# Raw V and R begun in one run behind psat, and two places of hand order made plain

## The chip, the cores and the metric

The kernel runs on one core of one Trainium2 chip. TensorE (PE; its weight loads are shown apart as PEld), the vector engine (DVE), ScalarE (ACT) and GpSimd (POOL) work beside each other, each through its own list of instructions; transfers are begun by a queue, here nearly always that of SyncE (SP), and carried out by 16 DMA engines. Engines wait for each other by semaphores. The metric is the device time of one execution in microseconds (us); a kernel's time is the median of its runs.

## The reference

Two blocks follow each other. The first is a recurrence over 768 steps for 4 batches and 8 heads with a state of 40 x 40; the second a mixture of four small networks over 3072 tokens.

```python
for t in range(S):                                   # B, H, S, D = 4, 8, 768, 40
    y[:, :, t] = einsum('bhd,bhde->bhe', r_t, state)
    Sa = einsum('bhde,bhe->bhd', state, a_t)
    state = state * w_t[:, :, None, :] - einsum('bhd,bhe->bhde', Sa, b_t)
    state = state + einsum('bhd,bhe->bhde', v_t, k_t)
x = y.transpose(0, 2, 1, 3).reshape(3072, 320)
p = probs / (probs.sum(-1) + 1e-9)
for e in range(4):
    out += p[:, e] * (relu(x @ w1[e]) @ w2[e])       # w1 320 x 1024, w2 1024 x 320
```

## The kernel before

**Units.** The 768 steps are cut into 12 chunks of 64; the four batches go two by two. A chunk of one pair is a unit, and there are 24, numbered u = 2 * chunk + pair. Within a unit the recurrence is written as matrix products; only a small state passes from a chunk to the next. The loop over u at line 1142 works on four units at once: it finishes unit u (`s`, from `step`), merges unit u+1 (`m`, from `merge`), prepares unit u+2 (`w`, from `within`) and loads unit u+3. `run(gen, n)` advances such a generator by n of its `yield`s.

**The parts of a unit, by the names in the profile.**
- `load_raw` (L206) begins the transfers of W, A, V and R in a blocked form (rawW, rawA, rawV, rawR, one buffer each); L223 is the line of the transfers. V and R take 8 moves each, 16 in all. They are put in a list, `later`, and begun from there by `begin_later`. `load` (L198) brings natW, natB, natK and natV.
- `within` (L402): DVE turns rawW into G (L241) and scans it (L439, then gl at L443), computes gp, its reciprocal, n_tok (L471) and k_tok (L476), turns rawA, rawV and rawR into AT, VT and RT (L241). PE transposes n_tok and k_tok (pNT, pKT, L79), and forms pfe, pc, pe, pev; ACT copies pfe to F (L506).
- `substitute` (L544) takes F into `blocks`, turns it into M (L555 to L571, DVE), and solves a triangular system by 16 rounds of multiply and add on POOL, in Z (L576 to L595).
- `merge` (L601): DVE turns Z into Qc (L606) and Qc into QTc (L608), POOL copies QTc to QT (L614), PE forms pY (from QTc) and pQ, ACT copies Yq and QT (L629).
- `step` (L638): prn and the copies RH (DVE, L656) and SN (ACT, L661); psat, SaT and SX; pxr, whose result DVE masks into SX (L400); pdy; Y (L733 and L738) and the state (L743, L744) on DVE; and the twelve SP transfers that lay Y out as the rows of x, xT (L762). `psat` is formed by the `run(s_next, 1)` at line 1238.

**The mixture.** A list `todo` holds its pieces: an `Up` is one half of x @ w1[e] (ph, 16 small and 16 large matmul records, then the ReLU to hs on ACT, L799), a down piece is a group of products with w2 or sums of it (p431, p75, p26, named p in the profile), added into osb by DVE (L833, L835). `add_h` forms the sums a of hs on DVE (L932). The weights w1p have two buffers; `used` begins the next load when a piece is done (L300). Channels 256 to 319 of x, the last ones, are the smaller tiles (`up_last`), the rest is `up_main`. An `Up` can be called (`lead`, that is the last channels first, then the main ones) or split into `begin` (main ones) and `end` (last channels, ReLU), with other work between. Two units with the same chunk share the pieces; only units 0 and 1 have their own (`mixture_of_unit`, L845). PE's accumulators for all of these share three PSUM banks (tag mm); the others share five (tag big).

**What sets the order.** Instructions of PE are kept in program order (`stated`, L70). On DVE, POOL and SP those marked `keep_in_program_order` keep their order among the marked ones; the others (Y, gp, RT, VT among them) are placed by a scheduler by its own estimate of when they can run. So a transfer's place in the program can change where DVE's instructions stand. [...]

**Where V and R are begun.** `mix(n)` (L1005) runs n pieces and begins three moves of `later` after each, or six after each if n is 1. In the main loop (u from 5 on) the 16 moves of a unit are appended at line 1222; the mix(2) at L1233 begins 6, the mix(2) at L1243 another 6, and the mix(2) at L1209 of the next pass the last 4. They are used by `turn_rv` in that next pass. In the passes with u below 5 the line `begin_later(len(later))` stands at the pass's start (L1159).

Of the kernel before, what the change touches and what calls it, by code (L numbers as in the profile page):

```python
# [15 lines left out]
def kernel(  # L16
# [58 lines left out]
    def matmul(**k):  # L75
        return stated(nc.tensor.matmul(**k))  # L76
# [158 lines left out]
    def go(moves, eng=None):  # L235
        for move in moves:
            move(eng or nc.sync)
# [65 lines left out]
    def used(n):  # L303

        while len(pieces) < n_pieces:
            k = len(pieces)
            if k in in_sums:
                before = k - 5 if k >= 5 else -1
            else:
                at = [x for x in range(k) if x not in in_sums]  # L310
                before = at[-2] if len(at) > 1 else -1
            if before >= n:
                break
            load_piece()

    def load_w2(e):
        tc.keep_in_program_order(nc.sync.dma_start(out=w2_sb[e][:], in_=moe_w2[e].rearrange("(f p) d -> p f d", p=P)))
# [451 lines left out]
    def up_banks(n):  # L769
        return [ps.tile([P, HF // 2, n], FP32, name="ph", tag="mm", bufs=3) for _ in range(2)]  # L770

    def up_last(k, xT, ph, opens):

        w1 = pieces[k]
        for f in range(HF // 2):
            for c in range(2):
                for i in range(2):
                    matmul(
                        out=ph[i][half(c), f, :], lhsT=w1.last[part(i), f, half(c)], rhs=xT[part(i), 2, :],
                        start=(opens and f == 0), stop=(not opens and f == HF // 2 - 1),  # L780
                    )
# [22 lines left out]
    class Up:  # L804
# [4 lines left out]
        def lead(self):  # L809
            if self.ph is None:  # L810
                self.ph = up_banks(self.n)
                up_last(*self.at, self.ph, True)
# [14 lines left out]
    def scale(q, e, minus=False):  # L827
        return (minus_gate if minus else gate)[:, q.c, q.bp, e:e + 1]

    def add(to, p, sc, start=False):  # L830

        if start:
            nc.vector.tensor_scalar(out=to, in0=p, scalar1=sc, scalar2=None, op0=ALU.mult)  # L833
        else:
            nc.vector.scalar_tensor_tensor(out=to, in0=p, scalar=sc, in1=to, op0=ALU.mult, op1=ALU.add)  # L835

    def store(q, osb, cols=slice(0, DM), second=nc.sync):
        for i, eng in enumerate((nc.sync, second)):
            row = q.b[i] * S + q.c * L
            eng.dma_start(out=out[row:row + L, cols], in_=osb[i * L:(i + 1) * L, cols])  # L840

    def outputs():
        return sb.tile([P, DM], FP32, name="osb", tag="osb", bufs=2)

    def mixture_of_unit(q):  # L845

        hs, at = {}, 2 * E * q.u

        def ups(e):
            hs[e] = []  # L850
            a, b = (Up(at + 2 * e + x, q.xT, P, hs[e].append) for x in range(2))

            def piece():
                a()
                b.begin()
                b.end()
                used(at + 2 * e + 2)
                if q.u == 0 and e + 2 < E:
                    load_w2(e + 2)

            piece.lead = a.lead
            return piece

        def down(e):
            po = ps.tile([P, DM], FP32, name="po", tag="mm", bufs=3)
            for f in range(NF):
                matmul(
                    out=po[:], lhsT=hs[e][f // HF][:, f % HF, 0:P], rhs=w2_sb[e][:, f, :],
                    start=(f == 0), stop=(f == NF - 1),
                )  # L870
            if e == 0:
                q.osb = outputs()
            add(q.osb[:], po[:], scale(q, e), e == 0)
            if e == E - 1:
                stores.append(lambda: store(q, q.osb))

        todo.append(ups(0))
        for e in range(E):
            todo.append(lambda e=e: down(e))
            if e + 1 < E:  # L880
                todo.append(ups(e + 1))
# [116 lines left out]
    todo, last, later, stores = [], [], [], []  # L998

    def begin_later(n):  # L1000
        for move in later[:n]:
            tc.keep_in_program_order(move(nc.sync))
        del later[:n]

    def mix(n):  # L1005

        for piece in todo[:n]:
            ready = stores[:]
            del stores[:]
            piece()  # L1010
            for begin_store in ready:
                begin_store()
            begin_later(3 if n > 1 else 6)
        del todo[:n]
# [5 lines left out]
    def open_next():  # L1020
        if not todo:
            return None
        piece = todo.pop(0)
        piece.begin()
        return piece

    def run(gen, n=99):
        if gen is None:
            return
        for _ in range(n):  # L1030
            if next(gen, gen) is gen:
                break
# [109 lines left out]
    for u in range(1, NU):  # L1142
        in_order[0] = True
        q = units[u]
        m = s_next = w = w_next = iter(())
        if u + 1 < NU:
            m, s_next = merge(units[u + 1]), begin_step(u + 1)
            w_next = ws[u + 1]
        if u + 2 < NU:
            w = ws[u + 2]  # L1150

        def gap(n, pieces=None):
            at = 4 * u + n
            run(sum_ops, sums_at.get(at, 0))
            mix((1 if at in sparse else 2) if pieces is None else pieces)

        early = u < EARLY
        if early:
            begin_later(len(later))  # L1159
            lead()  # L1160
            run(w_next)
            run(s, 1)
            gap(0)
            run(s, 1)
            run(w, 2)
            gap(1, 2 if u + 1 == EARLY else None)
            run(s)
            if u == 1:
                mixture_of_unit(q)
            elif q.bp:  # L1170
                mixture_of_chunk(units[u - 1:u + 1], chunks_x[q.c])
            go(load_raw(begin(u + 3), "WA"))
            load(units[u + 3], "WBKV")
            later.extend(load_raw(units[u + 3], "VR"))
            run(w, 2)
            soon = u > 1
            if soon:
                run(w, 1)
            run(m, 1)
            if soon:  # L1180
                substitute(units[u + 2], nc.gpsimd)
            gap(2)
            if not soon:
                run(w, 1)
                substitute(units[u + 2], nc.gpsimd)
            run(w, 1)
            ws.append(within(units[u + 3]))
            run(ws[u + 3], 1)
            run(m, 1)
            run(s_next, 1)  # L1190
            run(m)
            gap(3, 1)
            run(s_next, 1)
            s = s_next
            continue

        ahead = u + 3 < NU and u < EARLY + 3
        if ahead:
            go(load_raw(begin(u + 3), "W"))
        if u == EARLY:  # L1200
            run(w_next)
            lead()
        run(s, 1)
        run(w_next)
        lead()
        run(s)
        run(sum_ops, sums_at.get(4 * u, 0))
        run(w, 1)
        mix(2)  # L1209
        if q.bp:  # L1210
            mixture_of_chunk(units[u - 1:u + 1], chunks_x[q.c])
        begin_later(len(later))
        run(w, 1)
        run(m, 1)
        run(sum_ops, sums_at.get(4 * u + 1, 0))
        up = open_next()
        run(w, 1)
        mix(1)
        if u + 3 < NU:
            go(load_raw(units[u + 3] if ahead else begin(u + 3), "A" if ahead else "WA"))  # L1220
            load(units[u + 3], "WBKV")
            later.extend(load_raw(units[u + 3], "VR"))

        if up:
            up.end()
        run(s_next, 1)
        run(m, 1)
        run(w, 1)
        lead()
        if u + 2 < NU:  # L1230
            substitute(units[u + 2], nc.gpsimd)
        run(sum_ops, sums_at.get(4 * u + 2, 0))
        mix(2)  # L1233

        run(m, 1)
        run(w, 2)
        lead()
        run(s_next, 1)
        if u + 3 < NU:
            ws.append(within(units[u + 3]))  # L1240
            run(ws[u + 3], 1)
        todo[:2] = todo[1::-1]
        mix(2)  # L1243
        s = s_next
    while todo:
        mix(2)
        up = open_next()
        mix(1)
        if up:
            up.end()  # L1250
            lead()
    for piece in last:
        piece()

# [27 lines left out]
```

## Time and profile before

| | us |
|---|---|
| median of 3 runs | 1165.82 |
| range of the runs | 1164.3 to 1168.21 |
| profiled execution | 1169.21 |
| span of its trace | 1167.5 |
| PE busy | 1082.7 |
| DVE busy | 747.0 |
| POOL busy | 487.9 |

The span runs from the first to the last instruction of the profiled execution; the rest of its time lies around it. Busy times are of one engine, and they overlap. The groups of the page that concern the change are these; a row is line, engine, operation, output<-inputs, shapes and count, then busy us and mean ns of one, then the idle us just before them and what ended them:

```profile
L76 PE MATMUL ph<-xT,w1p 64*64 64x256 f32 (+3 forms) x3040 | 449.3, 385 | 6.2 <-PE ph L76 2.8
L582 POOL TENSOR_TENSOR Z<-M,Z 128x62 f32<-128x62 f32 (+7 forms) x352 | 160.6, 456 | 95.3 <-DVE M L571 69.5
L614 POOL COPY QT<-QTc 32x256 f32<-32x256 f32 x96 | 40.5, 422 | 331.3 <-DVE QTc L608 327.6
L76 PE MATMUL pY<-QTc,below 64*64 64x64 f32 x384 | 18.2, 240 | 37.8 <-DVE QTc L608 37.8
```

Idle time counts only on the engine that bounds the kernel; POOL's 331.3 us before QT are of no harm by themselves, PE's 37.8 us before pY may be. SPq and PEq stand for the queue of an engine (issuing or waiting), and "issue" is time in which an engine waited for nothing that the profile shows.

### The profile page before, as it was taken

To read this page: it belongs to the slowest core of one execution; us is meant where nothing else is said; L and a number is where in the kernel's file an instruction comes from. 1 tells how busy PE (TensorE), PEld (TensorE's weight loads), DVE (VectorE), ACT (ScalarE), POOL (GpSimd) and SP (SyncE) were. 2 spreads that over 40 slices of the span, in tenths; PEclk is the share of its full clock that TensorE was granted. 3 is DMA by queue.
4 is the path that set the end of the run, shared out by engine and by line. 5 is a ranking of instruction groups with operands and counts; after the bars stand their busy time and mean duration, and the time that the engine had idled before them with its cause. 6 is when DMAs were issued, how large, how long until landed. Compare 5 with 4: busy or idle time off the path is not lost.

```text
span 1167.5 us, 38490 instructions
## 1 busy us (share of the span) xinstructions
PE 1082.7 (93%) x16102; PEld 971.3 (83%) x16102; DVE 747.0 (64%) x1551; ACT 354.4 (30%) x956; POOL 487.9 (42%) x1274
## 2 busy tenths in 40 slices
PE   7789999989899899899899989989989999999998
PEld 6677788888789798798888878988978988898887
DVE  8766678797566665766668557766666675543343
ACT  2331434422224233233332233233232422321110
POOL 4116677745436245264362452643633624600000
PEclk8898999999899899999999999999999999999999
DMA  6875544542534434334344344354353342222220
GB/s 113 252 218 121 135 100 106 111 117 57 126 86 112 113 83 119 95 84 119 93 106 113 79 101 116 77 129 111 82 125 88 104 118 61 70 87 76 79 91 12
DMA packets 268868, 122.18 MB, mean 105 GB/s; under 512 B 213736, under 2 KB 242072, under 8 KB 268696
## 3 DMA queue, kind: packets, MB, share of 16 engines
q1 hardware_dynamic: 265416, 119.12, 40.5%
q8 instruction: 127, 2.08, 0.7%
q10 hardware_dynamic: 3280, 0.61, 0.3%
q14 instruction: 45, 0.37, 0.1%
HBM read 111.79 MB, written 3.93 MB: 99 GB/s over the span
## 4 chain that ended last, share of the span: by engine, by line
PE 61%; SPq 18%; DVE 12%; issue 4%; DMA 4%; ACT 1%; DVEq 0%; ACTq 0%
PE ph L76 26%; PE p L76 19%; SPq L762 10%; PE pdy L76 3%; SPq L223 3%; SPq L300 2%; DMA rawR<-in_r_dram 2%; PE psat L76 2%; PE pxr L76 2%; SPq L840 2%; PE pfe L76 1%; PE pY L76 1%; PE pQ L76 1%; PE po L76 1%; PE pc L76 1%
## 5 line engine op out<-in xcount | busy, mean ns | idle before, releaser
L76 PE MATMUL ph<-xT,w1p 64*64 64x256 f32 (+3 forms) x3040 | 449.3, 385 | 6.2 <-PE ph L76 2.8
L76 PEld LDWEIGHTS ph<-xT,w1p 128*128 128x128 f32 (+1 forms) x3040 | 341.8, 165 | 65.8 <-issue 16.3
L595 POOL TENSOR_TENSOR Z<-Z 128x31 f32<-128x31 f32 (+7 forms) x704 | 241.2, 343 | 55.2
L799 ACT ACTIVATE hs<-ph 128x512 f32<-128x512 f32 (+1 forms) x208 | 113.8, 564 | 384.5 <-PE ph L76 372.9
L582 POOL TENSOR_TENSOR Z<-M,Z 128x62 f32<-128x62 f32 (+7 forms) x352 | 160.6, 456 | 95.3 <-DVE M L571 69.5
L614 POOL COPY QT<-QTc 32x256 f32<-32x256 f32 x96 | 40.5, 422 | 331.3 <-DVE QTc L608 327.6
L932 DVE TENSOR_TENSOR a<-hs 128x512 f32<-128x512 f32 x220 | 147.8, 689 | 47.8 <-ACT hs L799 47.8
L76 PE MATMUL p<-sums,a 128*128 128x160 f32 x1056 | 164.9, 299 | 0.0
L835 DVE SCALAR_TENSOR_TENSOR osb<-p,gate,osb 128x320 f32<-128x320 f32 (+1 forms) x243 | 107.7, 478 | 83.9 <-PE p L76 81.8
L76 PEld LDWEIGHTS p<-sums,a 128*128 128x128 f32 x1056 | 152.8, 190 | 2.2
L76 PE MATMUL p<-w,hs 128*128 128x160 f32 x704 | 104.9, 302 | 0.6 <-DVE osb L835 0.6
L76 PE MATMUL p<-w,a 128*128 128x160 f32 x704 | 102.8, 299 | 0.0
L76 PEld LDWEIGHTS p<-w,hs 128*128 128x128 f32 x704 | 97.3, 190 | 2.3 <-issue 1.0
L76 PEld LDWEIGHTS p<-w,a 128*128 128x128 f32 x704 | 98.0, 190 | 0.0
L400 DVE COPY_PREDICATED SX<-mask_up,pxr 128x256 f32<-128x256 int32 x48 | 18.8, 442 | 60.2 <-PE pxr L76 60.2
L733 DVE TENSOR_TENSOR Y<-pdy,RS 128x256 f32<-128x256 f32 x44 | 16.7, 420 | 61.8 <-PE pdy L76 60.6
L457 ACT COPY NT<-pNT 128x512 f32<-128x512 f32 x24 | 14.1, 586 | 136.3 <-PE pNT L79 136.0
L76 PE MATMUL pY<-QTc,below 64*64 64x64 f32 x384 | 18.2, 240 | 37.8 <-DVE QTc L608 37.8
L451 DVE RECIPROCAL gp<-gp 128x320 f32<-128x320 f32 x24 | 51.4, 2142 | 0.1
L629 ACT COPY QT<-pQ 32x128 f32<-32x128 f32 x96 | 24.7, 257 | 82.2 <-PE pQ L76 81.1
L555 DVE STREAM_TRANSPOSE M<-blocks 128x1024 f32<-128x1024 f32 x24 | 47.3, 1971 | 3.0 <-ACT blocks L549 2.6
L76 PEld LDWEIGHTS pY<-QTc,below 64*64 64x64 f32 x384 | 15.4, 150 | 40.6 <-issue 39.7
(149 smaller groups left out, 1377.7 us busy)
## 6 DMA issues: line engine op xcount, KB each, us to landing
w1p<-in_moe_w_dram SPq DMA_DIRECT2D x95, 512.0 KB
w1p<-in_moe_w_dram SPq DMA_DIRECT2D x190, 64.0 KB
w<-in_moe_w_dram SPq DMA_DIRECT2D x4, 1280.0 KB
sums<-in_moe_w_dram SPq DMA_DIRECT2D x9, 512.0 KB
natW<-in_w_dram SPq DMA_DIRECT2D x48, 80.0 KB
natB<-in_b_dram SPq DMA_DIRECT2D x48, 80.0 KB
natK<-in_k_dram SPq DMA_DIRECT2D x48, 80.0 KB
out_dram<-osb SPq DMA_DIRECT2D x46, 80.0 KB
```

The source lines that it names most:

```text
L76: return stated(nc.tensor.matmul(**k))
L223: moves.append(lambda eng, out=t[o, n, 0:w_], in_=heads[:, hs, Q * y:Q * y + w_]: eng.dma_start(out=out, in_=in_))
L451: pin(nc.vector.reciprocal(out=gp[:], in_=gp[:]))
L555: ins = nc.vector.transpose(out=M[:], in_=cols)
L582: ins = eng.tensor_tensor(out=Z[:, 1:3, 0:n, j + 1:Q], in0=M[:, j:j + 2, None, j + 1:Q].to_broadcast([P, 2, n, m]), in1=Z[:, here, 0:n, j: ...
L595: eng.tensor_tensor(out=z[:, 0], in0=z[:, 0], in1=z[:, x], op=ALU.add)
L614: ins = nc.gpsimd.tensor_copy(out=q.QT[quarter(i), :, quarter(i % 2)], in_=QTc[quarter(i)])
L629: nc.scalar.copy(out=of_slot(to[quarter(2 * r)], y), in_=src)
L762: nc.sync.dma_start(out=xT[to:to + hi - lo, g, :], in_=Y[at:at + hi - lo, h // 2].rearrange("p i t -> p (i t)"),)
L799: nc.scalar.activation(out=h[:, i * HF // 2:(i + 1) * HF // 2, 0:n], in_=ph[i][:], func=ACTF.Relu,)
L835: nc.vector.scalar_tensor_tensor(out=to, in0=p, scalar=sc, in1=to, op0=ALU.mult, op1=ALU.add)
L932: nc.vector.tensor_tensor(out=t[:], in0=x, in1=y, op=op)
```

## The change

Three edits:
- In `mixture_of_unit` the second `Up` of a piece is called (last channels, then the main ones) where it was begun and ended (main ones, then the last channels).
- In the main loop, u from 5 on, all that is left in `later` is begun behind psat, that is ahead of the last mix(2) of the pass; so V's and R's 16 moves are all begun in one pass, and used in the next.
- The pieces left when the loop is over run in the order of the list, each `Up` called; before, every third was begun, another piece run, and then ended, with the last channels of the next one right behind.

```diff
@@ mixture_of_unit, ups, piece() (L853)
                 a()
-                b.begin()
-                b.end()
+                b()
                 used(at + 2 * e + 2)
@@ main loop (L1239)
         if u + 3 < NU:
             ws.append(within(units[u + 3]))
             run(ws[u + 3], 1)
+        begin_later(len(later))
         todo[:2] = todo[1::-1]
         mix(2)
         s = s_next
-    while todo:
-        mix(2)
-        up = open_next()
-        mix(1)
-        if up:
-            up.end()
-            lead()
+    mix(len(todo))
     for piece in last:
         piece()
```

`begin_later(n)` begins the first n moves of `later` on SP, each kept in program order, and takes them off the list.

## The prediction

> **What bounds the kernel now.** I read the page first (busy shares), then who waited for whom on TensorE (PE), then the timeline of one step of the main loop, then its queue view for the next step. The page says that PE is the bound as a whole: it is busy 1082.7 us of 1167.5. So only its 85 us of idle time can be won. The view of waits says where almost half of that idle time is.
>
> ```profile
> PE 1082.7 (93%) x16102; PEld 971.3 (83%) x16102; DVE 747.0 (64%) x1551; ACT 354.4 (30%) x956; POOL 487.9 (42%) x1274
> ...
> PE pY L76 <- DVE QTc L608: 37.8, 16, 5.4
> ...
> PE ph L76 <- PE ph L76: 2.8, 4, 0.7
> ```
>
> Sixteen times PE stands before pY until the vector engine (DVE) has turned QTc: 37.8 us. The step at 512 to 545 us shows why. Each row is start, duration, engine, line, names, and in brackets the idle time before it and what ended it.
>
> ```profile
> 512.33 0.78 DVE L400 COPY_PREDICATED SX<-mask_up,pxr 128x256 f32<-128x256 int32 x2 [2.95 <-PE pxr L76]
> 515.92 0.76 DVE L733 TENSOR_TENSOR Y<-pdy,RS 128x256 f32<-128x256 f32 x2 [2.81 <-PE pdy L76]
> 517.67 0.51 POOL L595 TENSOR_TENSOR Z<-Z 128x8 f32<-128x8 f32 x2
> 525.60 0.48 DVE L476 TENSOR_TENSOR k_tok<-natK,gp 128x320 f32<-128x320 f32 x1
> 527.93 0.60 PE L79 MATMUL pKT<-ident,k_tok 128*128 128x128 f32 x4
> 529.60 0.17 DVE L443 TENSOR_TENSOR gl<-gl,G 128x8 f32<-128x8 f32 x1
> 533.09 0.71 DVE L241 STREAM_TRANSPOSE RT<-rawR 128x512 f32<-128x512 f32 x1 [3.32 <-DMA rawR<-in_r_dram]
> 533.73 0.57 DVE L606 STREAM_TRANSPOSE Qc<-Z 128x256 f32<-128x256 f32 x1
> 534.34 0.45 DVE L608 STREAM_TRANSPOSE QTc<-Qc 128x256 f32<-128x256 f32 x1
> 534.93 0.59 PE L76 MATMUL pY<-QTc,below 64*64 64x64 f32 x13 [1.18 <-DVE QTc L608]
> 538.14 0.65 ACT L506 COPY F<-pfe 128x256 f32<-128x256 f32 x2
> 542.55 0.69 DVE L571 TENSOR_TENSOR M<-M,Z 128x512 f32<-128x512 f32 x1
> ...
> 564.53 0.52 POOL L595 TENSOR_TENSOR Z<-Z 128x8 f32<-128x8 f32 x2
> ```
>
> The raw R that DVE turns at 533.09 has been begun too late; DVE idles 3.32 us for it, and Qc and QTc stand behind it. The reader should also see two things that cost nothing yet: GpSimd (POOL) finishes Z, which Qc reads, only at 518.18, that is 2.3 us after Y has begun; and M at 543.24 is followed by a POOL chain that ends at 565.05. In the next step (560 to 581 us) the queue view adds this:
>
> ```profile
> 572.01 1.66 SPq L300 DMA_DIRECT2D w1p<-in_moe_w_dram  x3
> 573.72 1.53 SPq L223 DMA_DIRECT2D rawR<-in_r_dram  x3
> 575.36 2.45 SPq L840 DMA_DIRECT2D out_dram<-osb  x4
> ...
> 578.14 0.55 DVE L833 TENSOR_SCALAR osb<-p,gate 128x320 f32<-128x320 f32 x1 [3.73 <-DMA out_dram<-osb]
> ```
>
> In every second step DVE also waits for the output stores, since osb is written anew.
>
> [...] Qc's input Z was ready at 518.18, yet Qc ran at 533.73, right behind RT. [...] SP's 12 xT moves (L762) start only at 562.63, after Y of 560.56, and the stores stand behind them. [...] Here the POOL chain from M to Z's end takes 25.3 us where DVE adds the w2 sums (213.88 to 239.20) and 21.4 to 21.9 us later[...].
>
> **The change part by part.**
>
> *1. Raw V and R begun ahead.* Before, of the 16 moves per unit 12 go out in the two mix(2) at a step's end and 4 a step later. After, all 16 go out before the last mix, so the last four R moves (about 0.5 us each) leave SP some 20 us earlier, and R lands before the next step's SX. RT can then run as soon as its buffer is free, after pxr. From the built program I read the order of DVE: in the 16 steps from the Qc of 300.0 us to that of 990.6 us, RT, Qc and QTc now stand between SX and Y; before, they stood behind gl (L443). PE, ACT and POOL keep their order in these steps. That removes the wait before pY: 37.8 less the 2.35 us of the one at 251 us, so 35.4 us.
>
> *What is late next.* Qc needs Z. DVE now stops at Qc until POOL ends, and Y, the state, gp, n_tok, k_tok and all that follows stand behind it. In the steps from 370 us on Z ends 2.0 to 4.5 us after Y's present start. This closes a loop: Z end, Qc, QTc, Y, k_tok, pKT, pfe, F, M, the next Z. Its price, link by link:
> - Z's end to Y: Qc starts 0.03 us after Z (112.68 to 112.71 in an early step); from Qc's start to what follows QTc is 534.70 − 533.73 = 0.97. Sum 1.0.
> - Y's start to k_tok's end: 526.08 − 515.92 = 10.16. DVE has no gap in it, and it is 10.15 to 10.26 in the 15 steps from 278 to 929 us, so nothing of it shrinks.
> - k_tok to pKT's end: 0.75, from the one step where PE really waited for it (243.07 to 243.82).
> - pKT's end to F's end: 7.9, from the step with no wait before pY (987.88 to 995.78). It holds the p431 products, the last-channel products, prn, pY, pfe.
> - F to M: 4.46 in every step. M to Z's end: 21.8.
>
> That is 46.1 us a turn. In every second step the stores come between: xT goes out from Y+2.1, w1p from Y+11.1 (median of the rows), the stores from Y+12.8 once the three R moves no longer stand before them, and the first osb follows 2.8 us behind its store's issue, at Y+15.6; the second 1.5 us later at Y+17.1. The rest of osb takes 1.2, so RH starts at Y+18.3. The ACT copies SN wait for RH and stand before F, which ends 2.6 us after RH's start (536.17 to 538.79), at Y+20.9 against Y+18.8 in the other steps. With 4.46, 21.6 and 1.0 the turn is 48.0 us. A mean of 47.05.
>
> Before, from the SX end of 325.44 to that of 971.40, 14 steps took 46.14 each, of which about 2.1 were the wait before pY. So PE would need 44.0, but the loop asks for 47.05. Walking it: Y of the first changed step starts at 281.50 + 1.0 = 282.5 (278.05 before). Fifteen turns follow, eight of 48.0 and seven of 46.1, less 0.3 for a first chain of 21.33: the last of these Y starts at about 988.6 (973.66 before), and its pfe ends 10.16 + 0.75 + 6.2 later at 1005.7 (994.03 before). So part 1 costs +11.7 us. PE's idle time moves from pY to pKT, and to the ph whose bank waits for DVE's osb.
>
> SP: the ten moved DMAs take about 5 us of issue, between the V moves and the next w1p. In the window at 550 to 557 us SP is idle for 5 us, waiting for PE's ph; that hides them. Without that cover w1p would be late by as much, but its packets ended about 4 us after issue (526.75 to 530.6) and PE uses them 5.7 us after that (536.3), so 0 to 3 us in all. I take 0.
>
> *2. begin/end becomes b() for units 0 and 1.* Eight pieces; the same 16 + 16 matmuls, the last channels first. For it: bank 0 gets its ReLU half a main (1 us) earlier, worth at most one ReLU of 0.3 us each. Against it: the last-channel products need both banks at once, so they may wait for the ReLU of the piece before, and the last-channel weights, which are begun after the main ones, are needed first. The trace shows such a bank wait as 1.31 us once at 213 us. Bounds −2 to +3 us over eight; I take 0.
>
> *3. The left-over pieces in plain order.* In the tail end() is followed at once by lead() of the next piece, which waits for the ReLU of the bank just ended: the row "PE ph <- PE ph", 4 times 0.7. In plain order the p431 products lie between. DVE frees the p75 bank about 0.5 us before the new ph needs it (1101.80 against 1102.3), so no new wait is due. −2.8 us, bounds −3 to +1.
>
> Sum: +11.7 + 0 − 2.8 = +8.9 us. The profiled execution took 1169.2 us (span 1167.5 and 1.7 around it), 3.4 over the median of 1165.8; the sum is put on the median: **1174.7, so 1175**.
>
> **Rivals.**
> - *Z does not hold DVE* (POOL runs earlier than its spans say, or the loop has slack I don't see). Then all of 35.4 + 2.8 us is won: about 1128. For it: the removed wait is real and large. Against: Z's end is seen to release Qc within 0.03 us in early steps, and in all steps from 250 us on it comes after Y's need. It decides where Z ends at least 4 us sooner against SX than now. Chance 0.11.
> - *The loop binds, but the store wait adds nothing.* All turns 46.1: the last Y at 973.3, pfe at 990.4, so −3.6, with the tail −6.4: 1159. For it: ACT might take F without being held by RH. Against: ACT's list has SN before F, and SN follows RH in every step read. Chance 0.15; values between this and the forecast are "no change".
> - *Slower than the forecast:* the late DVE also delays SP (xT, then w1p, then the stores), and PE waits for weights. It decides once w1p's issue slips more than about 5 us against PE's use. At 1 us more a turn: 15 us more, 1190. Against: xT and w1p are tied to Y, and pKT, which PE needs before that w1p, is tied to Y as well. Chance 0.14.
> - *The change doesn't do what it says:* R still lands after SX. SP would have to be held before the R moves; their buffer is free since the RT of the same step. Under 0.02, in the first.
>
> **How the numbers follow.** The forecast has 0.60, with a range of its own of 1169 to 1182: an error of 0.3 us a turn is 4.5 us, and parts 2 and 3 give −2 to +7. I can't tell less than 0.3% (3.5 us) from no change. Faster: the first rival and most of the second, 0.20. Within 0.3%: the rest of it and the low end of the forecast, 0.12. Slower: 0.68. The range leaves out the first rival and the far end of the third: 1156 to 1190.
>
> **What would show it.** Right: no row "PE pY <- DVE QTc" after 300 us; DVE idle before Qc, released by POOL Z, 2 to 7 us in each of 16 steps; Y beginning 1.0 us after Z's end; steps alternating near 46 and 48 us; PE waiting for k_tok and for osb; the tail's four gaps of 0.7 gone. Wrong: Z ending before SX; RT still released by a DMA; SN copied without RH; or steps near 44 us.

## The result and the profile after

| | before | after |
|---|---|---|
| median of 11 runs each, us | 1166.53 | 1171.97 |
| range of the runs, us | 1160.72 to 1169.83 | 1167.96 to 1175.21 |
| span of the profiled execution, us | 1167.5 | 1171.8 |

The changed kernel is slower by 0.49%: the ratio of the times is 1.0049, with a 95% interval of 1.0028 to 1.0069. That is 5.4 us between the medians, where 8.9 were forecast.

The first fence is from the page of the changed kernel: TensorE's busy time, and the shares of the engines in the chain that ended last.

```profile
PE 1090.9 (93%) x16102; PEld 973.6 (83%) x16102; DVE 749.2 (64%) x1551; ACT 355.4 (30%) x956; POOL 483.6 (41%) x1274
...
PE 33%; POOL 24%; DVE 23%; issue 7%; ACT 5%; SPq 4%; DMA 3%; DVEq 0%; POOLq 0%; ACTq 0%
```

The second line of the same part of the page of the kernel before:

```profile
PE 61%; SPq 18%; DVE 12%; issue 4%; DMA 4%; ACT 1%; DVEq 0%; ACTq 0%
```

PE is as busy as ever, at 93%, but the chain tells of another bound: POOL, which does not appear in the line of before, now carries 24% of it. The view of waits of the changed kernel, PE first and then DVE (who waited, for whom, us in all, times, longest), says where:

```profile
PE ph L76 <- DVE osb L835: 36.7, 16, 3.0
...
PE pY L76 <- DVE QTc L608: 2.3, 1, 2.3
```

```profile
DVE Qc L606 <- POOL Z L595: 87.9, 17, 5.6
...
DVE osb L833 <- DMA out_dram<-osb: 21.1, 11, 4.8
```

The row of that last wait of DVE in the kernel before:

```profile
DVE Qc L606 <- POOL Z L595: 3.4, 3, 1.9
```

PE's wait before pY has gone from 37.8 us to a single one, at 250 us. In its place PE waits 36.7 us for osb, 16 times, in a row that did not exist. And DVE waits 87.9 us for Z where it waited 3.4 us. The step from 508 us on, the same unit as the step shown for the kernel before, in the timeline (start, duration, engine, line, names, the idle time before it and what ended it):

```profile
508.89 0.78 DVE L400 COPY_PREDICATED SX<-mask_up,pxr 128x256 f32<-128x256 int32 x2 [2.95 <-PE pxr L76]
509.56 0.70 DVE L241 STREAM_TRANSPOSE RT<-rawR 128x512 f32<-128x512 f32 x1
514.21 0.51 POOL L595 TENSOR_TENSOR Z<-Z 128x8 f32<-128x8 f32 x2
514.76 0.63 DVE L606 STREAM_TRANSPOSE Qc<-Z 128x256 f32<-128x256 f32 x1 [4.50 <-POOL Z L595]
515.42 0.45 DVE L608 STREAM_TRANSPOSE QTc<-Qc 128x256 f32<-128x256 f32 x1
515.79 0.71 DVE L733 TENSOR_TENSOR Y<-pdy,RS 128x256 f32<-128x256 f32 x2
520.81 1.89 PE L76 MATMUL ph<-xT,w1p 128*128 128x256 f32 x8
523.78 1.97 PE L76 MATMUL ph<-xT,w1p 128*128 128x256 f32 x8 [1.08 <-DVE osb L835]
525.51 0.48 DVE L476 TENSOR_TENSOR k_tok<-natK,gp 128x320 f32<-128x320 f32 x1
531.74 0.57 PE L76 MATMUL pY<-QTc,below 64*64 64x64 f32 x13
```

RT no longer waits for R: it runs right behind SX. Qc, next in DVE's list, then stands 4.50 us until POOL has ended Z, and Y, whose inputs pdy and RS were done by 512.58, runs only at 515.79, behind QTc and 1.03 us after Qc's start. Everything behind it is late, so that PE stops in the middle of a ph, whose second bank DVE has not yet emptied into osb (1.08 us at 523.78). When pY comes (531.74), QTc has been there for 16 us. The wait was moved, not removed.

From the Y of 280.53 us to that of 985.27 us fifteen turns took 46.98 us each; the same fifteen took 46.37 us each in the kernel before (Y of 278.05 to Y of 973.66; the 46.14 of the prediction leaves out the first of them).

### The profile page after: what moved, and what is told of

Read it like the earlier page. It is cut to its first block, busy times and chain, and to the rows that moved or that the text cites. A ratio compares the mean times of both kernels' runs of the same rounds, so it can differ in the third digit from the quotient of the medians.

```text
span 1171.8 us, 38502 instructions
## 1 busy us (share of the span) xinstructions
PE 1090.9 (93%) x16102; PEld 973.6 (83%) x16102; DVE 749.2 (64%) x1551; ACT 355.4 (30%) x956; POOL 483.6 (41%) x1274
## 4 chain that ended last, share of the span: by engine, by line
PE 33%; POOL 24%; DVE 23%; issue 7%; ACT 5%; SPq 4%; DMA 3%; DVEq 0%; POOLq 0%; ACTq 0%
POOL Z L595 15%; PE ph L76 13%; PE p L76 10%; POOL Z L582 10%; DVE M L555 3%; DVE a L931 3%; DVE gp L451 3%; DVE osb L835 2%; ACT Yq L629 2%; DMA out_dram<-osb 2%; PE po L76 2%; SPq L762 1%; SPq L223 1%; ACT blocks L549 1%; DVE Z L567 1%
## 5 line engine op out<-in xcount | busy, mean ns | idle before, releaser
L76 PE MATMUL ph<-xT,w1p 64*64 64x256 f32 (+3 forms) x3040 | 454.4, 382 | 45.5 <-DVE osb L835 36.7
L76 PEld LDWEIGHTS ph<-xT,w1p 64*64 64x64 f32 (+1 forms) x3040 | 338.5, 164 | 111.5 <-issue 65.1
L595 POOL TENSOR_TENSOR Z<-Z 128x31 f32<-128x31 f32 (+7 forms) x704 | 236.1, 335 | 55.2
L582 POOL TENSOR_TENSOR Z<-M,Z 128x62 f32<-128x62 f32 (+7 forms) x352 | 156.1, 444 | 95.1 <-DVE M L571 69.3
L552 POOL COPY below<-F 32x256 f32<-32x256 f32 x48 | 21.1, 439 | 311.3 <-ACT F L506 309.6
L614 POOL COPY QT<-QTc 32x256 f32<-32x256 f32 x96 | 46.0, 479 | 83.1 <-DVE QTc L608 73.0
L606 DVE STREAM_TRANSPOSE Qc<-Z 128x256 f32<-128x256 f32 x24 | 15.0, 623 | 88.0 <-POOL Z L595 87.9
L549 DVE COPY blocks<-F 32x256 f32<-32x256 f32 x48 | 16.8, 350 | 38.2 <-ACT F L506 37.8
```

Source lines behind the costliest of these rows:

```text
L549: tc.keep_in_program_order(move(out=blocks[quarter(i)], in_=q.F[quarter(i), :, quarter(i % 2)]))
L552: tc.keep_in_program_order(nc.gpsimd.tensor_copy(out=q.below[quarter(i)], in_=q.F[quarter(i), :, 0:Q]))
L582: ins = eng.tensor_tensor(out=Z[:, 1:3, 0:n, j + 1:Q], in0=M[:, j:j + 2, None, j + 1:Q].to_broadcast([P, 2, n, m]), in1=Z[:, here, 0:n, j: ...
L595: eng.tensor_tensor(out=z[:, 0], in0=z[:, 0], in1=z[:, x], op=ALU.add)
L614: ins = nc.gpsimd.tensor_copy(out=q.QT[quarter(i), :, quarter(i % 2)], in_=QTc[quarter(i)])
```

## The experiments

Each was run beside the kernel before on the same chip; ratios are against that.

**1. The early loads alone.**

```diff
+        begin_later(len(later))
         todo[:2] = todo[1::-1]
         mix(2)
```

> Kernel before with the added begin_later alone; pieces and tail as before. Theory (DVE stops at Qc until GpSimd ends Z, a loop of about 47 us a turn): the whole kernel's loss less the tail's gain, so +2.8 us on the changed kernel, about 1175, +7 to +10 us on the kernel before; DVE waits for POOL Z about 85 us in all before Qc, and none of PE's waits at pY is left after 300 us; the four 0.7 us gaps of PE at the end are still there. Rival (the loss comes from the pieces or the tail): no slower than the kernel before, by at most the 35 us of the pY waits faster.

Measured: 1170.4 us, ratio 1.0043 (1.0027 to 1.0059). DVE waits 90.7 us for Z before Qc, PE 37.5 us for osb and 2.3 us once before pY. The turn is 46.99 us. So this one line makes the whole new profile, and its +5 us (0.43%) are most of the result; that is less than the 7 to 10 us expected. DVE's waits for the stores at L833 are half of the changed kernel's (10.2 us against 21.1) at the same turn, which is a first sign that these waits add little to it.

**2. The tail alone.**

```diff
-    while todo:
-        mix(2)
...
+    mix(len(todo))
```

> Kernel before with the left-over pieces in plain order alone. Theory: -2.8 us (four gaps of 0.7 us 'PE ph <- PE ph' go), so about 1163.5 beside a before of 1166.5. Rival (the plain order makes a new wait for DVE's osb or for weights): 0 to +2 us.

Measured: 1164.9 us, ratio 0.9985 (0.9968 to 1.0002), about 1.7 us less. Three of the four gaps of 0.7 us are gone, and no new wait of PE stands in their place. The first of the four (at 1075.67 us before, 1076.08 here) stays. The interval just includes no change; the sign is the expected one, and three gaps come to 2.1 us where 2.8 were expected.

**3. The pieces of units 0 and 1 alone.**

```diff
-                b.begin()
-                b.end()
+                b()
```

> Kernel before with b() in place of begin and end for units 0 and 1 alone. Theory: 0 (-2 to +3 us), and SX of step 7 ends within 1 us of the kernel before. Rival (this is what brought the early phase 1.3 us forward in the changed kernel, SX of step 7 at 274.50 against 275.80): -1.3 us, carried to the end or swallowed by the loop after.

Measured: 1169.64 us, ratio 1.0023 (1.0007 to 1.0039), about +2.7 us: slower, near the upper end of what was allowed for. SX of step 7 ended at 274.65 us (275.80 before), so the eight pieces themselves did not take longer in that execution; the loss appears later, in a loop whose order on PE, DVE, POOL and SP is that of the kernel before. I did not find its place: the start of the loop differs by more than this between executions of programs that are the same up to there (SX of step 7 at 275.80 before, 271.02 in experiment 2, 269.51 in experiment 6).

The three parts add up: 0.43 − 0.15 + 0.23 = 0.51%, against 0.49% measured for all.

**4. RT, Qc and QTc put later in DVE's list.** The loads stay early. The turns of V and R are marked so that they keep their program order behind AT; Qc and QTc, which are traced behind RT, follow. The edit moves VT too: in the changed kernel it stands ahead of SX, here right ahead of RT. In the two traces the lists of ACT, POOL and SP have the same order, and DVE's differs only in these four and in the turns to G and the product of AT and G that they pass.

```diff
-                    turn_raw(t[:], n["raw" + x][:])
+                    pin(turn_raw(t[:], n["raw" + x][:]), q.apart)
```

> Changed kernel with the turns of V and R kept in program order behind AT for the later units, so that DVE runs Y, the state, k_tok and AT*G first and only then RT, Qc, QTc, some 12 us after Y's start, still ahead of pY; loads, SP and pieces unchanged. Theory (what costs is DVE standing at Qc): DVE's 88 us before Qc and PE's 37 us at ph for osb go almost wholly, Z ends some 2 us after Y's start and releases nobody; the turn falls from 47.0 to PE's own 44.0 to 44.8, so the kernel comes to 1128 to 1142 us. Rival (the early loads on SP, or the stores, hold the turn): it stays within 4 us of the changed kernel's 1172, with the waits moved to other rows.

Measured: 1111.11 us, ratio 0.9518 (0.9492 to 0.9545). The kernel is 4.8% faster than before, and below the range that was expected. The timeline of this version, one step:

```profile
528.72 0.78 DVE L400 COPY_PREDICATED SX<-mask_up,pxr 128x256 f32<-128x256 int32 x2 [2.95 <-PE pxr L76]
531.77 0.76 DVE L733 TENSOR_TENSOR Y<-pdy,RS 128x256 f32<-128x256 f32 x2 [2.27 <-PE pdy L76]
535.73 0.51 POOL L595 TENSOR_TENSOR Z<-Z 128x8 f32<-128x8 f32 x2
541.44 0.48 DVE L476 TENSOR_TENSOR k_tok<-natK,gp 128x320 f32<-128x320 f32 x1
543.99 0.67 DVE L241 STREAM_TRANSPOSE RT<-rawR 128x512 f32<-128x512 f32 x1
544.59 0.59 DVE L606 STREAM_TRANSPOSE Qc<-Z 128x256 f32<-128x256 f32 x1
545.35 0.40 DVE L608 STREAM_TRANSPOSE QTc<-Qc 128x256 f32<-128x256 f32 x1
549.41 0.57 PE L76 MATMUL pY<-QTc,below 64*64 64x64 f32 x13
```

Z ends at 536.24, 4.5 us after Y began, and nobody waits for it: DVE has Y, the state and k_tok to do first. QTc is done at 545.75, 3.7 us ahead of pY. DVE's wait before Qc is 3.9 us in all, none of it from 300 us on; the row "PE ph <- DVE osb" has gone from PE's waits. A turn is now 42.85 us (Y at 274.63 to 917.45 in 15 turns). The page says of PE:

```profile
PE 1067.5 (96%) x16102; PEld 959.3 (86%) x16102; DVE 744.3 (67%) x1551; ACT 355.0 (32%) x956; POOL 499.3 (45%) x1274
```

The same 16102 matmul records take 15.2 us less than in the kernel before, and 23.4 less than in the changed one. The part on the clock, below, explains most of this.

**5. A longer chain on POOL, twice:** in the changed kernel, and in the version of experiment 4.

```diff
+            if j == Q - 2 and q.apart and not at_once:
+                for _ in range(3):
+                    eng.tensor_copy(out=Z[:, 1], in_=unit_cols[:])
             n, m = j // 4 + 1, Q - 1 - j
```

> Changed kernel with three more GpSimd copies of 128x256 into Z's scratch part just before the last step of each chain of the later units (0.4 us each, so 1.2 us more from M to Z's end; the result is unchanged; every other order as in the changed kernel). Theory (the loop through Z, Y, F and M sets the turn): each of about 15 turns grows by 1.2 us, so +17 to +20 us on the changed kernel, about 1190. Rival (the turn is set by PE, by the osb banks or by SP and Z only seems to release Qc): 0 to +4 us, with DVE's wait for Z taking up what would otherwise be another wait.

> The same three GpSimd copies a chain in the version with RT, Qc and QTc behind AT. Theory: Z ends 3 to 4.5 us after Y's start there and is read 12 us after it, so 1.2 us more costs nothing: 0 to +2 us on 1111. Rival (GpSimd work costs by itself[...]): +10 us or more, as in the changed kernel.

Measured: 1205.52 us, ratio 1.0341 (1.0309 to 1.0372), in the changed kernel; 1111.89 us, ratio 0.9532 (0.9511 to 0.9553), in the other, where it costs less than the runs can tell, though the chain grew there by 1.3 to 2.1 us. So GpSimd's chain sets the turn of the changed kernel, and not of the other. But the price was higher than expected: 33.5 us over the changed kernel's 1171.97, where 17 to 20 were expected. The turn went from 46.98 to 48.93. The chain from M to Z's end grew by 1.33 us (22.53 against 21.20); the rest, 0.6 us a turn, is of the kind that the waits show (the edit adds three lines, so L609 here is L606 of the other listings):

```profile
PE ph L76 <- DVE osb L838: 61.3, 16, 4.3
```

```profile
DVE Qc L609 <- POOL Z L598: 113.0, 18, 6.9
```

PE's gap in ph is longer, and its clock halves behind 14 of these 16 gaps. The fifteen turns make 29 of the 33.5 us.

**6. The edit of experiment 4 without the early loads,** that is in the kernel before. There RT, Qc and QTc stand late already, behind gl, and stay there; only VT moves, from ahead of SX to behind AT.

> Kernel before with only the turns of V and R kept in program order behind AT for the later units, loads as before. RT still follows gl and waits for the late R. Theory (both are needed, an early R and an order in which DVE doesn't meet Z too soon): within 3 us of the kernel before, 1163 to 1170, the waits of PE at pY still 33 to 44 us. Rival (the order alone brings the gain): 1111 to 1125.

Measured: 1167.16 us, ratio 1.0016 (1.0002 to 1.003). In the waits of this kernel:

```profile
PE pY L76 <- DVE QTc L608: 43.1, 17, 5.9
```

The wait of the kernel before is all there. So neither the move of VT nor a late place of RT gains anything while R itself comes late, and by experiment 1 an early R gains nothing while RT stands ahead of Y. The gain needs both: R early, and RT, Qc and QTc behind Y and k_tok. (The two edits together, without the other parts of the change, are the second run of experiment 8.)

**7. Three osb buffers in the changed kernel.**

```diff
-        return sb.tile([P, DM], FP32, name="osb", tag="osb", bufs=2)
+        return sb.tile([P, DM], FP32, name="osb", tag="osb", bufs=3)
```

> Changed kernel with three osb buffers for two. Theory (in every second step the stores hold osb, RH, SN and F): DVE's 21 us of waits for the stores at L833 shrink to under 5, and the eight store turns, 47.1 to 48.5 us, come to that of the others, 45.5 to 47.1: -6 to -12 us, about 1162. Rival (other waits of the same turn end as late, the half clock or PE's ph for one): within 3 us of the changed kernel's 1172.

Measured: 1167.86 us, ratio 1.0011 (0.9997 to 1.0024), about 4 us under the changed kernel, between what was expected (6 to 12) and the rival (within 3). DVE's waits show two changes:

```profile
DVE VT L241 <- DMA rawR<-in_r_dram: 21.3, 9, 5.8
...
DVE osb L833 <- DMA out_dram<-osb: 6.9, 5, 2.5
```

The wait for the stores shrinks by 14 us, nearly as far as expected, and a wait of VT for R grows from 8.0 to 21.3 us. The second need not cost anything: VT stands ahead of SX and Qc, and in experiment 1 its waits for V and R came to 25.1 us, against 19.5 in the changed kernel, at the same turn. The turn is 46.68 us, only 0.3 under the changed kernel's: F's delay behind the stores falls from 9.4 to about 5 us in the fifteen turns, and in seven of them pKT is still 1.3 to 1.6 us late, with PE at half its clock (below).

**8. The version of experiment 4, part by part.** Without the new order of the pieces of units 0 and 1; with neither this nor the plain tail; and once more as it was.

> The version with RT, Qc and QTc behind AT, with the pieces of units 0 and 1 as in the kernel before (begin and end in place of b()). Theory from the run of that part alone (+0.23% there, not explained): 2 to 3 us faster than 1111, about 1108.5. Rival (the part is worth nothing and the +0.23% came of where the main loop happened to stand): within 1.5 us of 1111.

> Kernel before with the early loads and RT, Qc and QTc behind AT alone: pieces and tail as before. Theory: the tail's four gaps of 0.7 us are back, so 2 to 3 us slower than the version with begin and end for units 0 and 1 and the plain tail. Rival: the tail is worth nothing here, within 1 us.

> The version with RT, Qc and QTc behind AT once more, to stand beside the two others on one chip: 1109 to 1112.5 us, as before.

Measured, in this order: 1107.28 us (ratio 0.9489, 0.9465 to 0.9514), 1109.41 us (0.9502, 0.9478 to 0.9527), 1109.14 us (0.9506, 0.9483 to 0.953). The intervals overlap. The differences of 2 us have the expected sign in both comparisons, but these runs don't separate them. The version with the lowest median, with the early loads, the later turns, the plain tail and the old order of the first units' pieces, takes 5.1% less than the kernel before.

## Why the prediction was right, and which of its terms were not

**The mechanism was right.** The wait before pY went, except the one at 251 us. DVE stops at Qc in each of the 16 steps, released by Z, and Y begins 1.06 to 1.13 us after Z's end (1.0 was taken). Experiment 4 takes away this stop, and the loss with it; beside RT, Qc and QTc its edit moves VT past the same neighbours, and that move alone gained nothing in experiment 6. Experiment 5 lengthens POOL's chain, and the kernel pays for it only where DVE stands at Qc. The rival in which Z does not hold DVE would have been 1128. It fell. So did the one of late weights: PE's waits name no DMA of the weights, and no cost of SP shows. One wait for a transfer did grow: VT now waits 19.5 us in all for V and R. It stands ahead of SX and Qc, where DVE then waits for Z in any case. Two signs that were named did not come: the turns don't alternate near 46 and 48 us (three take 45.5, the others 46.8 to 48.5), and PE's waits have no row for k_tok, only that for osb.

**The turn was right in sum only.** It was forecast at a mean of 47.05 us and measured at 46.98. Its links, from the same start and end points in the trace of the changed kernel:

| link | forecast | measured |
|---|---|---|
| Z's end to Y | 1.0 | 1.06 |
| Y to k_tok's end | 10.16 | 10.20 |
| k_tok to pKT's end | 0.75 | 0.71 in 7 turns, 1.9 to 2.3 in 8 |
| pKT's end to F's end, turns without stores and with pfe in time | 7.9 | 7.89 |
| F to M | 4.46 | 4.46 |
| M to Z's end | 21.8 | 21.20 |
| the stores, mean over all turns | 0.95 | 0.63 |

The links without the stores come to 45.52 us where 46.1 was forecast; the 0.6 is POOL's chain, taken from steps in which DVE worked beside its end. In the changed kernel DVE stands still for the last 4.1 to 5.6 us of it. The chain takes 21.3 to 21.9 us before, 20.9 to 21.2 after, and again 21.6 to 21.9 in experiment 4, where DVE works on. The traces show the same, shape by shape, for DVE operations with two inputs in SBUF: POOL's multiply Z<-M,Z of 128x70 takes 0.33 us in the changed kernel at 511.83 us, beside nothing on DVE, and 0.84 us in experiment 4 at 532.70 us, beside the operation that forms Y from Y and G. In all 13 traces, from 300 us on, the 126 records of this shape with no such operation beside them take 0.32 to 0.33 us, those beside an operation with one input in SBUF included; the 82 with one beside them have a median of 0.76 us.

The stores cost 9.4 us in 15 turns, unevenly; forecast was 1.9 in each of the eight turns that have them. In the four of these in which pKT came in time they cost 1.3, 2.9, 2.9 and 1.3 us, a mean of 2.1. In the four in which pKT came late they cost 0 to 0.8. So the price of a store wait was about right, but in half of the turns it lay under another delay, the next one.

And one term was missing: the clock. In 8 of the 15 turns pKT came 1.2 to 1.6 us late, 11.7 us in all, and 1.1 us more were lost between pKT and pfe: 12.8 us, or 0.85 a turn. In these turns the matmuls of ph ahead of pKT ran at half the clock (0.53 granted from 569.30 to 572.85 us, in the section on the hardware). 45.52 + 0.63 + 0.85 = 47.0. Two terms too large and one not there cancelled, so that the agreement of the sum within 0.1 us is luck.

**The start.** The first changed Y came at 280.53, not 282.5; 1.3 of these 2 us are already in SX of step 7 (274.50 against 275.80), before the new order on DVE has delayed anything. As experiment 3 showed, that start moves by some microseconds between executions. The last Y of the loop was 11.6 us late, where 14.9 were forecast: 2.0 from the start, 1.3 from the turns. pfe then ended at 1002.34, 8.3 us later than before (11.7 forecast), and the next Y at 1026.50, 7.1 later. From there to the end the trace has 145.3 us against 148.1.

**The tail.** Those 2.8 us are the number that was forecast for it, but not its doing alone. Three of the four gaps went, 2.1 us, in the changed kernel as in experiment 2; and the kernel before has a spell of half clock at 1018.92 us, for which the changed one has none from 904 us to the span's last 2 us. By itself the tail gave about 1.7 us, and its interval includes 0.

**Part 2** was taken at 0 within −2 to +3, and measured +2.7 us alone. The bound held; the value was wrong, and the cause is open. (The 1.31 us at 213 us, which the prediction reads as a wait for a bank, stand in the view as "issue": the profile names no cause for them.)

**PE's own turn** was taken for 44.0 us, that is 46.14 less 2.1 of waiting. Experiment 4 shows 42.85. Of the difference, an estimated 0.7 us is again the clock (half of the 20.5 us of half clock that the kernel before has in those 14 turns, by turn), and the rest is not accounted for: removing a wait also removes what follows from it. This did not touch the forecast of the change, as the loop stood above both, but it did touch the rival: with Z out of the way the kernel is at 1111, not at 1128. "Only its 85 us of idle time can be won", the prediction's first reading of the page, was wrong for the same reason: experiment 4 also won 15.2 us of PE's busy time.

## What the runs showed of the hardware

**An idle gap on PE can be paid twice.** In the changed kernel, the eight large matmuls of one bank of ph before and after a gap, in PE's timeline:

```profile
564.48 1.89 PE L76 MATMUL ph<-xT,w1p 128*128 128x256 f32 x8
...
569.32 3.54 PE L76 MATMUL ph<-xT,w1p 128*128 128x256 f32 x8 [2.95 <-DVE osb L835]
```

The table by stretches (from and to, length, busy time and count of each engine, then the granted TensorE clock, the DMA share and GB/s) for the same two groups:

```profile
564.50:566.40 1.90, 1.87 (x10) 1.31 (x8) 1.90 (x2) 0.00 (x0) 0.00 (x0) 1.00 0.08 22
569.30:572.85 3.55, 3.53 (x9) 2.73 (x10) 3.55 (x8) 0.00 (x0) 0.00 (x0) 0.53 0.11 25
```

The same work takes 1.65 us more: the clock granted was 0.53 in the second stretch and 1.00 in the first. Wherever such a spell of half clock stands between 270 and 960 us, in any trace here, it lasts 3.41 us or twice that. Within a trace all spells begin whole multiples of 3.413 us apart (381.81, 429.59 and 487.62 us in the changed kernel are 14 and 17 of them apart).

What went ahead of a spell can be counted. The length of a gap tells only a part. Between 270 and 960 us of all 13 traces, 37 of the 38 gaps of 3.08 us or more were followed by a spell, 30 of the 52 from 1.9 to 3.08 us, and one of the 22 from 1.2 to 1.9 us. PE's idle share tells more, when the time is cut into slices of 3.413 us whose borders the spells mark. The traces have 2548 such slices at full clock between 270 and 960 us. Of these, 68 were followed by a slice at half clock, and PE had been idle for 57% or more of each; in the other 2480 it had been idle for 57% or less. So the slices ahead of a spell were not all idle as a whole. By an estimate from these counts (57% of 3.413 us), a gap alone had to put some 1.95 us into one slice; one of 3.23 us in experiment 3, which fell across a border, had no spell behind it. This is read from the traces, with the ends of matmuls as the profile models them; no run moved a gap to try it.

In the kernel before, the spells between 298 and 862 us come to 27.3 us. Half of that, about 13.7 us, is an estimate of what they cost, close to the 15.2 us by which PE's busy time falls in experiment 4, which has no spell from 270 to 960 us. "Busy" therefore is no measure of the work: the same number of matmul records was busy for 1067.5, 1082.7 and 1090.9 us in three kernels.

## What to carry to other kernels

When a late input is mended, look at what stands next to it in the same engine's list and for what that waits in turn: here DVE only changed R for Z, and the early load paid once its reader and those behind it were placed after the work that the others needed first. Work the new loop out link by link before trusting it: that found the stop at Z, and most links within 0.1 us, though the sum agreed by luck. Take each link from steps in which the same engines work beside it. And count a gap on TensorE at more than its length: here 67 of the 90 gaps of 1.9 us or more were followed by a spell of half clock, and the one shown above added 1.65 us to a gap of 2.95.
